# Turning gathered token rows on VectorE by way of DRAM, instead of on TensorE, for experts two to seven

## The chip, the core and the metric

The program runs on one NeuronCore of a Trainium2 chip. The metric is the device time of one execution in microseconds (us), the median of three. The engines are TensorE (PE: matrix products; PEld: its weight loads), VectorE (DVE), ScalarE (ACT), GpSimd (POOL) and SyncE (SP, which here only issues DMAs). Each works through its own instructions in order and waits on semaphores; DMAs are issued from an engine's queue and land later.

## The reference, cut to what matters

```python
# attention: B, S, D = 8, 2496, 256; d_qk = 64
scores = scale * np.matmul(z, z.transpose(0, 2, 1))
attn = np.maximum(scores, 0.0) ** 2
x = (u * np.matmul(attn, v)).reshape(B * S, D)
# mixture of experts: E, F = 8, 1024
do_compute = x @ w_skip > 0
e_idx = np.argmax(xc @ w_gate, axis=1)          # xc = x[do_compute]
gate_w = softmax(xc @ w_gate)[e_idx]
for e in range(E):
    h = np.maximum(xc[mask] @ w1[e], 0.0)       # mask = e_idx == e
    y[mask] = gate_w[mask, None] * (h @ w2[e])
out[do_compute] = xc + y                        # the other tokens keep x
```

All is float32. About half of the 19968 tokens are computed, 1073 to 1502 for each expert.

## The kernel before

**Attention phase (to about 1250 us).** It is tiled by batch and by 512 queries. The rows x are stored in DRAM (`xr`) and the routing scatters every computed token's number and gate into its expert's list (`lst`). The change does not touch this phase.

**Expert phase.** The experts, counted here from 0 to 7 as in the code (e0 to e7), come one after the other. An expert's tokens are taken in *pairs* of two tiles of 128. Each product is split into float32r high and low parts (`xh`/`xl`, `w1h`/`w1l`, `hh`/`hl`). `unit` computes 256 to 512 tokens: it forms h in PSUM (tile `psh`), ACT takes the relu into `hh`, DVE the rest into `hl`, PE multiplies by w2 into `y`, DVE adds x and POOL scatters the rows to `out`. The first NFIX = 3 pairs of each expert are *fixed units*. What is left is done in one arm of a switch (`tc.Switch`), chosen by the expert's count: its code is entered by a branch on each engine. Weights of expert e + 1 are brought by SP (`raw`), cast on ACT and subtracted on POOL (`w1l`, `w2t`), in eight pieces over the fixed units of expert e.

**A pair's way before.** `fetch` gathers its rows by two indirect DMAs of POOL (tiles `xgf` for pairs 0 to 2, `xgu` for later ones); before them DVE copies the row numbers (`go`). `turn_pe` transposes it on PE with four products against an identity into PSUM (`pst`); ACT casts it into xh and DVE subtracts for xl. Turned pairs lie in `xt` (two buffers in turn) and `xtf` (pair 0 of an expert from e1 on).

**What sets the order.** The instruction order is the code's (`manual_schedule`). `unit` runs a list of parts: for a fixed unit h0, h1, h2, h3, y0, y1, then the rest of y. `fills` maps a part's number to the steps written behind it. At 3 the next pair is turned. In the third unit (i = 2) pair 4 is turned at 5 and pair 0 of the next expert at 7, the last thing before the switch. The pieces of the weights stand at 1, 3 and 5.

Of the kernel before, what the change touches and what calls it, by code (L numbers as in the profile page):

```python
# [8 lines left out]
F32 = mybir.dt.float32  # L9
# [35 lines left out]
def f32(ap):  # L45
    return ap.bitcast(F32)
# [3 lines left out]
def attn_moe(ctx, tc, zT, uT, v, wg, w1, w2, cst, pad, out):  # L50
# [4 lines left out]
    nc = tc.nc  # L55
# [593 lines left out]
    def turn_pe(xg, xt, n=2, o=0, rows64=False):  # L649

        if rows64:
            ps = spare()[:, 0, :].rearrange("p (d q) -> p d q", d=2)
        else:
            ps = ps_acc.tile([P, 2, 2 * P], F32, name="pst", tag="acc")
        for t in range(n):
            for d in range(2):
                nc.tensor.transpose(ps[:, d, t * P : (t + 1) * P], xg[:, t, d * P : (d + 1) * P], ident)  # L657
        xh, xl = (x[:, :, o : o + n * P] for x in xt)
        nc.scalar.copy(xh, ps[:, :, : n * P])
        nc.vector.tensor_sub(xl, ps[:, :, : n * P], f32(xh))  # L660

    def unit(e, hw, ids, xg, xt, fills=(), own=False, lead=3):


# [320 lines left out]
    def add(fills, *slots):  # L985
        for k, f in slots:
            fills.setdefault(k, []).append(f)

    def rows(e, i):
        return lambda: fetch(ids_of(e, i), pair(e, i))  # L990

    for e in range(E):
        more = e + 1 < E
        wq = load_w(e + 1, nc.gpsimd if e else nc.vector) if more else []
        narms = NARM + (2 if e == 0 else 1)
        for i in range(NFIX):
            fills = {}
            if e:

                add(fills, (1, rows(e, i + 3)), (3, lambda: turn_pe(pair(e, i + 1), turned(e, i + 1))))  # L1000
                if e == 1 and i == 0:
                    add(fills, (0, rows(1, 2)))
                if more:
                    add(fills, (4, rows(e + 1, i)))
                if i == 0 and e + 2 < E:
                    add(fills, (6, lambda: load_ids(idts[e + 2], e + 2, 2 * NSTAT)))
                add(fills, *zip((1, 3, 5), wq[3 * i : 3 * i + 3]))
            elif i == 0:
                add(fills, (0, lambda: turn_pe(pair(0, 1), turned(0, 1))))
                add(fills, (1, gates), (1, logits), (1, route), (2, counts), (2, gate), (2, rows0), (2, rows1),  # L1010
                    (2, store), (4, store), (5, end_routes), (6, end_lists))
                add(fills, *zip((0, 2), left))
            elif i == 1:
                add(fills, (1, end_counts), (3, lambda: turn_pe(pair(0, 2), turned(0, 2))), (4, rows(0, 3)), (6, rows(0, 4)))
                add(fills, *zip((1, 3, 5), wq[:3]))
            else:
                add(fills, (1, rows(1, 0)), (3, rows(0, 5)), (4, lambda: turn_pe(pair(0, 3), turned(0, 3))),
                    (5, rows(1, 1)), (6, lambda: load_ids(idts[2], 2, 2 * NSTAT)))
                add(fills, *zip((1, 2, 3, 5, 6), wq[3:]))
            if more and i == NFIX - 1:  # L1020
                add(fills, (7, lambda: turn_pe(pair(e + 1, 0), turned(e + 1, 0))))
            if i == NFIX - 1:

                add(fills, (5, lambda: turn_pe(pair(e, NFIX + 1), turned(e, NFIX), 2, 2 * P)))
                n = nc.values_load(fin["arm"][0:1, e : e + 1], min_val=0, max_val=narms - 1)
                add(fills, (1, lambda: tc.switch_hint({g: n for g in ENGINES}, narms, label="rest%d" % e)))
            ids = ids_of(e, i) if e else idt_e[:, 2 * i : 2 * i + 2, :]
            xg = pair(e, i)
            unit(e, 4, ids, [xg[:, 0, :], xg[:, 1, :]], turned(e, i), fills)


        for arm in tc.Switch(n, narms, hint="rest%d" % e):
            ws = widths(arm) if arm <= NARM else []
            if arm > NARM:
                for i in range(NFIX):
                    xg = fetch(ids_of(0, i), xgs["u"][i])
# [3 lines left out]
            i, there = NFIX, NFIX + 2  # L1040
            for j, hw in enumerate(ws):
                fills = {}
                after = ws[j + 1 :]
                nxt = i + -(-hw // 4)
                while there < min(i + 3, end - 1):
                    there += 1
                    add(fills, (1, rows(e, there)))
                if after:
                    xt = xts[(NFIX + j + 1) % 2]
                    add(fills, (3, lambda nxt=nxt, xt=xt: turn_pe(pair(e, nxt), xt)))  # L1050
                    if after[0] > 4:
                        add(fills, (5, lambda nxt=nxt, xt=xt: turn_pe(pair(e, nxt + 1), xt, 2, 2 * P)))
                w = -(-hw // 2)
                xg = [pair(e, i + t // 2)[:, t % 2, :] for t in range(w)]
                unit(e, hw, ids_of(e, i, w), xg, xts[(NFIX + j) % 2], fills, not more and not after, 3 if j else 4)
                i = nxt
            if arm >= NARM:
                ce = nc.values_load(fin["cnt"][0:1, e : e + 1], min_val=0, max_val=N)
                with tc.For_i((NSTAT if arm == NARM else NFIX) * UT, ce, UT) as tok:
                    it = op.tile([P, 2, 2], I32, name="it", tag="it")  # L1060
                    nc.sync.dma_start(
                        it, lst[bass.ds(tok + e * CAP, UT), :].rearrange("(k p) c -> p k c", p=P)
                    )
                    xg = fetch(it, xgs["u"][0])
                    turn_pe(xg, xts[0])
                    unit(e, 4, it, [xg[:, 0, :], xg[:, 1, :]], xts[0])


# [53 lines left out]
```

## Time and profile before

| what | value |
|---|---|
| time, median of 3 runs | 1735.2 us (1734.55 to 1735.56) |
| profiled execution | 1747.08 us, of which the span is 1745.1 us |
| PE busy | 1724.1 us, 99% |
| VectorE busy | 1206.2 us, 69% |
| ScalarE busy | 1112.6 us, 64% |
| POOL busy | 520.1 us, 30% |
| granted TensorE clock | 0.996 |
| HBM | 184.21 MB read, 136.02 MB written |

Shares are averages over two unlike phases. In the expert phase PE works on; DVE and ACT are busy about 40% and a third of the time, POOL over half. A row of the timeline gives start, duration, engine, line, operation, out<-in, and in brackets the idle time before it and what ended it. A row with a count at the end (x4) is several instructions in one, from the first's start to the last's end. In the chain of waits a row is start, duration and what the end of the program hung on then; "issue" there is time in which an engine waited for nothing that the profile shows. SPq is a DMA's issue on SP.

### The profile page before, as it was taken

The page shows a single profiled execution, that of the slowest core. Times are in us where ns is not written, and L with a number is a line of the kernel's source. Part 1 is how long each engine was busy: PE and PEld are TensorE (multiplying, and loading weights), DVE is VectorE, ACT ScalarE, POOL GpSimd, SP SyncE. Part 2 cuts the span into 40 slices and gives each one's busy share as a digit, 9 for nine tenths or more (in the row PEclk, how much of TensorE's full clock was granted, in tenths as well). Part 3 has the DMA queues.
Part 4 walks back from the last instruction along what each step waited for, and adds up shares of the span by engine and source line. Part 5 has one row for each costly group of instructions (what it writes and reads, how often), then busy time and mean ns, then how long its engine had stood idle before and what let it go on. Part 6 is the DMA issues. An engine that isn't in the chain of part 4 may idle for free.

```text
span 1745.1 us, 39255 instructions
## 1 busy us (share of the span) xinstructions
PE 1724.1 (99%) x15474; PEld 1537.9 (88%) x15474; DVE 1206.2 (69%) x1976; ACT 1112.6 (64%) x1409; POOL 520.1 (30%) x516
## 2 busy tenths in 40 slices
PE   9999999999999999999999999999989999999998
PEld 7888789988888998888889888888889999999997
DVE  6877877887887888788788878877744334443333
ACT  7877877787687778768777876877333333333321
POOL 1103213212211321231132023112446556635731
PEclk9999999999999999999999999999999999999999
DMA  5576699579858957985895799589543323322210
GB/s 179 152 203 193 151 247 281 144 211 258 236 146 243 277 147 204 272 239 146 236 262 162 207 261 254 140 225 250 149 111 84 90 83 106 100 61 86 86 42 26
DMA packets 408113, 303.29 MB, mean 174 GB/s; under 512 B 202768, under 2 KB 346001, under 8 KB 407152
## 3 DMA queue, kind: packets, MB, share of 16 engines
q1 hardware_dynamic: 393728, 276.37, 57.6%
q0 software_dynamic: 13632, 22.99, 4.7%
q8 instruction: 137, 2.24, 0.5%
q14 instruction: 184, 1.51, 0.3%
q10 hardware_dynamic: 432, 0.18, 0.0%
HBM read 184.21 MB, written 136.02 MB: 183 GB/s over the span
## 4 chain that ended last, share of the span: by engine, by line
PE 90%; DMA 3%; issue 3%; DVE 1%; ACT 1%; another core or an unknown queue 1%; POOL 1%; SPq 0%; POOLq 0%; DVEq 0%; ACTq 0%
PE acc L419 59%; PE y L710 10%; PE psh L691 10%; PE ps L302 8%; DMA out<-o,idt 2%; PE psm L491 1%; PE pst L657 1%; PE ps L285 0%; DMA kept<-rt 0%; DVE hl L697 0%; DVE al L390 0%; DMA raw<-in_v 0%; ACT ah L386 0%; DMA xgu<-xr,go 0%
## 5 line engine op out<-in xcount | busy, mean ns | idle before, releaser
L419 PE MATMUL acc<-ah,vh 64*128 64x512 f32 (+1 forms) x3120 | 643.7, 384 | 0.9 <-DVE ah L386 0.8
L419 PE MATMUL acc<-ah,vl 64*128 64x512 f32 (+1 forms) x3120 | 629.4, 383 | 0.0
L390 DVE TENSOR_TENSOR al<-r,ah 128x1024 fp32r<-128x1024 f32 (+1 forms) x400 | 479.8, 1206 | 135.2 <-ACT ah L386 114.9
L419 PE MATMUL acc<-al,vh 64*128 64x512 f32 (+1 forms) x3120 | 499.0, 383 | 0.6 <-DVE al L390 0.2
L590 POOL DMA_INDIRECT lst<-pair,dest x160 | 202.4, 1265 | 773.5 <-DVE dest L588 688.7
L386 ACT CAST ah<-r 128x1024 fp32r<-128x1024 f32 (+1 forms) x356 | 363.5, 1032 | 90.4 <-PE acc L419 41.8
L419 PEld LDWEIGHTS acc<-ah,vh 64*128 64x128 f32 x3120 | 329.3, 185 | 48.1 <-DVE ah L386 1.6
L419 PEld LDWEIGHTS acc<-ah,vl 64*128 64x128 f32 x3120 | 329.6, 185 | 41.6 <-DVE vl L122 0.3
L419 PEld LDWEIGHTS acc<-al,vh 64*128 64x128 f32 x3120 | 312.5, 184 | 51.0 <-DVE al L390 7.7
L376 ACT ACTIVATE r<-ps 128x1024 f32<-128x1024 f32 (+1 forms) x224 | 228.0, 1018 | 134.6 <-PE ps L302 116.1
L696 ACT ACTIVATE hh<-psh 128x512 fp32r<-128x512 f32 (+2 forms) x172 | 96.3, 572 | 287.6 <-PE psh L691 233.1
L377 ACT ACTIVATE r<-r 128x1024 f32<-128x1024 f32 (+1 forms) x224 | 236.3, 1055 | 7.1
L710 PE MATMUL y<-w2t,hh 128*128 128x256 f32 (+1 forms) x1328 | 235.8, 280 | 0.0
L697 DVE SCALAR_TENSOR_TENSOR hl<-psh,hh 128x512 fp32r<-128x512 f32 (+2 forms) x172 | 110.0, 655 | 151.9 <-ACT hh L696 121.3
L319 DVE STREAM_TRANSPOSE rt<-r 128x512 f32<-128x512 f32 x304 | 197.4, 688 | 10.2 <-DMA kept<-rt 9.4
L710 PEld LDWEIGHTS y<-w2t,hh 128*128 128x128 f32 (+1 forms) x1328 | 201.1, 186 | 1.8 <-issue 0.6
L691 PE MATMUL psh<-xt,w1h 128*128 128x256 f32 (+3 forms) x896 | 185.8, 304 | 8.6 <-DVE hl L697 5.9
L710 PE MATMUL y<-w2t,hl 128*128 128x256 f32 (+1 forms) x664 | 184.8, 278 | 0.8 <-DVE hl L697 0.7
L691 PEld LDWEIGHTS psh<-xt,w1h 128*128 128x128 f32 x896 | 142.4, 190 | 14.5 <-DVE hl L697 7.3
L691 PE MATMUL psh<-xt,w1l 128*128 128x256 f32 (+3 forms) x448 | 135.3, 302 | 0.0
L742 POOL DMA_INDIRECT out<-o,idt x77 | 76.5, 994 | 167.6 <-DVE o L739 132.5
L710 PEld LDWEIGHTS y<-w2t,hl 128*128 128x128 f32 (+1 forms) x664 | 123.0, 185 | 1.2 <-DVE hl L697 1.2
(197 smaller groups left out, 1750.6 us busy)
## 6 DMA issues: line engine op xcount, KB each, us to landing
kept<-rt SPq DMA_DIRECT2D x242, 256.0 KB
r<-kept SPq DMA_DIRECT2D x90, 512.0 KB
r<-kept SPq DMA_DIRECT2D x62, 448.0 KB
raw<-in_v SPq DMA_DIRECT2D x80, 256.0 KB
ut<-in_uT SPq DMA_DIRECT2D x32, 512.0 KB
xr<-xrow SPq DMA_DIRECT2D x128, 128.0 KB
out<-xr SPq DMA_DIRECT2D x32, 512.0 KB
raw<-in_w SPq DMA_DIRECT2D x64, 256.0 KB
```

Source lines behind the costliest of these rows:

```text
L302: nc.tensor.matmul(to, k[h, o : o + P], queries(ci, q, h, n), start=(m == 0), stop=(m == 2))
L319: nc.vector.transpose(t[:, :, 32 * k : 32 * k + 32].rearrange("p (k a) i -> p a k i", k=4), r[:, x, :].rearrange("p (a k i) -> p a k i", a ...
L376: nc.scalar.activation(r[:, :, :n], ps[:, :, :n], AF.Relu, scale=isc)
L377: nc.scalar.activation(r[:, :, :n], r[:, :, :n], AF.Square)
L386: (nc.scalar.copy if on_act(ci, p) else nc.vector.tensor_copy)(h_, r_)
L390: nc.vector.tensor_sub(l_, r_, f32(h_))
L419: nc.tensor.matmul(acc[t][:, :n], w[h, x, dd], a[h, x, :n], start=(first and t not in halves[:m]), stop=(last and t not in halves[m + 1 :]),)
L590: put = nc.gpsimd.indirect_dma_start(out=lst, out_offset=bass.IndirectOffsetOnAxis(ap=dest[:, t : t + 1], axis=0), in_=pair[:, t, :], in_o ...
L691: nc.tensor.matmul(ps[:, j * W : (j + 1) * W], wt[:, a, o : o + P], x[:, d, :W], start=(m == 0), stop=(m == 5),)
L696: nc.scalar.activation(hh[:, : G * W], ps[:, : G * W], AF.Relu)
L697: nc.vector.scalar_tensor_tensor(hl[:, : G * W], ps[:, : G * W], 0.0, f32(hh[:, : G * W]), op0=ALU.max, op1=ALU.subtract)
L710: nc.tensor.matmul(ys[t], h[:, tt], w2t[f][:, k, :], start=(f == 0 and m == 0 and t % share == 0), stop=(f == NF - 1 and m == 2), skip_gro ...
```

## The change

For experts from FAR = 2 on, a pair is no longer turned by PE. SP writes the gathered rows to a DRAM buffer (`far`, one for each pair and each parity of e) and reads them back with four DMAs as 32-row blocks that lie across partitions (`blocks`, into `blk`, or into `xgu` number 2 for pair 0). DVE transposes all 32x32 blocks in one instruction (`turn_dve`, into `xraw`); cast and subtraction stay, but read SBUF in place of PSUM. The columns come out in another order, and w1 is reordered on the host to match.

The gathers of a pair stand in other fills: two pairs in each fixed unit as before, but pairs 3 and 4 of the own expert in unit 0, pair 5 and the next expert's pair 0 in unit 1, the next expert's pairs 1 and 2 in unit 2. Expert 1 gathers pair 5 only if its arm wants it. Each write and each reading of blocks has a place of its own in the fills.

```diff
+FAR = 2
...
+    far = [[dram.tile([UT, D], F32, name="far%d%d" % (k, i)) for i in range(NSTAT)] for k in range(2)]
...
+    def blk_of(i):
+        return blk[i % 2][:, : UT // 32] if i else xgs["u"][2].rearrange("p t (m f) -> p (t m) f", f=64)
+
+    def blocks(e, i):
+        src = far[e % 2][i].rearrange("(m i) (b f) -> b i m f", i=32, b=4)
+        for b in range(4):
+            nc.sync.dma_start(blk_of(i)[32 * b : 32 * b + 32], src[b])
+
+    def to_far(e, i):
+        return lambda: nc.sync.dma_start(far[e % 2][i].rearrange("(t p) d -> p t d", p=P), pair(e, i))
+
+    def turn_dve(e, i, xt, o=0):
+        raw = zp.tile([P, 2 * D], F32, name="xraw", tag="zf", bufs=3)
+        nc.vector.transpose(
+            raw.rearrange("p (d m i) -> p m d i", d=2, i=32),
+            blk_of(i).rearrange("p m (d j) -> p m d j", d=2),
+        )
+        xh, xl = (x[:, :, o : o + UT] for x in xt)
+        r = raw.rearrange("p (d q) -> p d q", d=2)
+        nc.scalar.copy(xh, r)
+        nc.vector.tensor_sub(xl, r, f32(xh))
...
     def pair(e, i):
-        return xgs["f"][NFIX * (e % 2) + i] if i < NFIX else xgs["u"][i % 4]
+        if e < FAR:
+            return xgs["f"][NFIX * (e % 2) + i] if i < NFIX else xgs["u"][i % 4]
+        j = i % (NFIX + 3)
+        if j < NFIX:
+            return xgs["f"][NFIX * (e % 2) + j]
+        return xgs["u"][j % 4] if e % 2 else more_rows[j - NFIX]
...
+    def turn(e, i, xt, o=0):
+        return (lambda: turn_dve(e, i, xt, o)) if e >= FAR else (lambda: turn_pe(pair(e, i), xt, 2, o))
...
-                add(fills, (1, rows(e, i + 3)), (3, lambda: turn_pe(pair(e, i + 1), turned(e, i + 1))))
+                if e < FAR:
+                    if i < NFIX - 1:
+                        add(fills, (1, rows(e, i + 3)))
+                else:
+                    add(fills, (0, to_blocks(e, i + 1)))
+                    if i == 0:
+                        add(fills, (0, to_far(e, 2)), (1, rows(e, 3)), (4, rows(e, 4)))
+                    elif i == 1:
+                        add(fills, (1, to_far(e, 3)), (1, rows(e, 5)), (4, to_far(e, 4)))
+                    else:
+                        add(fills, (1, to_blocks(e, 4)), (3, to_far(e, 5)), (6, to_blocks(e, 5)))
+                add(fills, (3, turn(e, i + 1, turned(e, i + 1))))
...
-                if more:
-                    add(fills, (4, rows(e + 1, i)))
+                if more and i == 1:
+                    add(fills, (3, rows(e + 1, 0)))
+                if more and i == 2:
+                    add(fills, (0, to_far(e + 1, 0)), (1, rows(e + 1, 1)), (4, to_blocks(e + 1, 0)),
+                        (4, rows(e + 1, 2)), (6, to_far(e + 1, 1)))
...
             if more and i == NFIX - 1:
-                add(fills, (7, lambda: turn_pe(pair(e + 1, 0), turned(e + 1, 0))))
+                add(fills, (7, turn(e + 1, 0, turned(e + 1, 0))))
...
+    w1 = np.concatenate([moe_w1[:FAR], moe_w1[FAR:, cols]])
```

In the arms the same steps are put in for pairs from 6 on, and a loop for very large counts is adapted.

**On SP**, in the fixed units of e3 (raw: the next expert's weights; idt5: a list; far12: pair 2 of an odd expert; far00: pair 0 of the next, even one), from unit 0 on, before:

```order
L97 DMA raw_40508<-in_w1 128x512
L97 DMA raw_40546<-in_w2 128x512
L631 DMA idt5_206<-lst_88 128x16x2
L97 DMA raw_40629<-in_w2 128x512
L97 DMA raw_40676<-in_w2 128x512
L97 DMA raw_40716<-in_w2 128x512
```

and now, from the last weights of unit 1 to the end of unit 2:

```order
L99 DMA raw_40797<-in_w2 128x512
L677 DMA far14_101<-xgu_18280 128x2x256
L99 DMA raw_40830<-in_w2 128x512
L1081 TENSOR_LOAD arm_18550
L1081 ISA x2
L674 DMA blk_18285<-far13_100 32x8x64 x4
L677 DMA far00_89<-xgf_17860 128x2x256
L674 DMA blk_18284<-far14_101 32x8x64 x4
L1082 SWITCH_STRIDE
L1082 ISA
L1082 BRANCH_PREFETCH_HINT
L677 DMA far15_102<-xgu_18281 128x2x256
```

The weights' last load is now ahead of the blocks of pair 3, and the write of the next expert's pair 0 (far00) ahead of the blocks of pair 4 (far14); behind far15 follow the four reads of far00.

**On POOL**, in unit 1 of e3 (xgu: the own expert's later pairs; xgf: the next expert's), before:

```order
L639 DMA xgu<-xr,go 128x256 x2
L153 TENSOR_TENSOR w1l<-raw,w1h 128x512
L159 TENSOR_TENSOR w2t<-raw,w2t 128x256 x2
L639 DMA xgf<-xr,go 128x256 x2
L159 TENSOR_TENSOR w2t<-raw,w2t 128x256 x2
L742 DMA out<-o,idt_204 19968x256 x2
```

and now:

```order
L641 DMA xgu<-xr,go 128x256 x2
L155 TENSOR_TENSOR w1l<-raw,w1h 128x512
L641 DMA xgf<-xr,go 128x256 x2
L161 TENSOR_TENSOR w2t<-raw,w2t 128x256 x4
L771 DMA out<-o,idt_220 19968x256 x2
```

The number of gathers is the same; the xgf pair, which was pair 1 of the next expert and is now its pair 0, went ahead of one piece of w2t.

**On DVE**, the end of unit 2 of e3, before:

```order
L660 TENSOR_TENSOR xt_17848<-pst,xt_17848 128x2x256
L637 COPY go<-idt_205 128x2
L660 TENSOR_TENSOR xt_17848<-pst,xt_17848 128x2x256
L660 TENSOR_TENSOR xtf<-pst,xtf 128x512
L739 SCALAR_TENSOR_TENSOR o<-y,idt_204,xgf 128x256 x2
```

and now:

```order
L689 TENSOR_TENSOR xt_17864<-xraw,xt_17864 128x2x256
L639 COPY go<-idt_221 128x2
L682 STREAM_TRANSPOSE xraw<-blk 128x8x2x32
L689 TENSOR_TENSOR xt_17864<-xraw,xt_17864 128x2x256
L682 STREAM_TRANSPOSE xraw<-xgu 128x8x2x32
L689 TENSOR_TENSOR xtf<-xraw,xtf 128x512
L768 SCALAR_TENSOR_TENSOR o<-y,idt_220,xgf 128x256 x2
```

The transposes of pair 4 and of the next expert's pair 0 (read from xgu number 2, where its blocks are put) stand in DVE's queue ahead of the third unit's output and of the branch.

More of the change, by code (lines that the diff above doesn't have):

```diff
@@ L928, in attn_moe @@
     row_tiles("u", 4)
+    blk += [xp.tile([P, QC // 32, D // 4], F32, name="blk", tag="xrow") for _ in range(2)]
+    more_rows += [xp.tile([P, 2, QC], F32, name="xgx", tag="ut", bufs=3)[:, 0].rearrange("p (t f) -> p t f", t=2) for _ in range(3)]
     xtf += [zp.tile([P, 2, 2 * P], F32R, name="xtf", tag="zl", bufs=ZBUFS) for _ in range(2)]
@@ L1008, in attn_moe @@
             elif i == 0:
-                add(fills, (0, lambda: turn_pe(pair(0, 1), turned(0, 1))))
+                add(fills, (0, turn(0, 1, turned(0, 1))))
                 add(fills, (1, gates), (1, logits), (1, route), (2, counts), (2, gate), (2, rows0), (2, rows1),
@@ L1013, in attn_moe @@
             elif i == 1:
-                add(fills, (1, end_counts), (3, lambda: turn_pe(pair(0, 2), turned(0, 2))), (4, rows(0, 3)), (6, rows(0, 4)))
+                add(fills, (1, end_counts), (3, turn(0, 2, turned(0, 2))), (4, rows(0, 3)), (6, rows(0, 4)))
                 add(fills, *zip((1, 3, 5), wq[:3]))
             else:
-                add(fills, (1, rows(1, 0)), (3, rows(0, 5)), (4, lambda: turn_pe(pair(0, 3), turned(0, 3))),
+                add(fills, (1, rows(1, 0)), (3, rows(0, 5)), (4, turn(0, 3, turned(0, 3))),
                     (5, rows(1, 1)), (6, lambda: load_ids(idts[2], 2, 2 * NSTAT)))
@@ L1039, in attn_moe @@
             end = NFIX + -(-sum(ws) // 4)
-            i, there = NFIX, NFIX + 2
+            i, there = NFIX, NFIX + 2 - (e == 1)
             for j, hw in enumerate(ws):
@@ L1046, in attn_moe @@
                     there += 1
-                    add(fills, (1, rows(e, there)))
+                    add(fills, (1, rows(e, there)), *([(3, to_far(e, there))] if e >= FAR else []))
                 if after:
                     xt = xts[(NFIX + j + 1) % 2]
-                    add(fills, (3, lambda nxt=nxt, xt=xt: turn_pe(pair(e, nxt), xt)))
-                    if after[0] > 4:
-                        add(fills, (5, lambda nxt=nxt, xt=xt: turn_pe(pair(e, nxt + 1), xt, 2, 2 * P)))
+                    for k in range(2 if after[0] > 4 else 1):
+                        if e >= FAR and nxt + k > NFIX + 2:
+                            add(fills, (2 + 2 * k, to_blocks(e, nxt + k)))
+                        add(fills, (3 + 2 * k, turn(e, nxt + k, xt, 2 * P * k)))
                 w = -(-hw // 2)
@@ L1063, in attn_moe @@
                     )
-                    xg = fetch(it, xgs["u"][0])
-                    turn_pe(xg, xts[0])
+                    xg = xs = fetch(it, xgs["u"][2 if e >= FAR else 0])
+                    if e >= FAR:
+                        xs = zp.tile([P, 2, D], F32, name="xs", tag="zf", bufs=3)
+                        for t in range(2):
+                            nc.vector.tensor_copy(
+                                xs[:, t].rearrange("p (d b j) -> p b d j", d=2, b=4),
+                                xg[:, t].rearrange("p (b d j) -> p b d j", b=4, d=2),
+                            )
+                    turn_pe(xs, xts[0])
                     unit(e, 4, it, [xg[:, 0, :], xg[:, 1, :]], xts[0])
```

7 lines of the change are left out of this document (5 added, 2 removed).

## The prediction

> **What bounds the kernel now.** I read the page first, then the matrix engine's waits from 1230 us on, then the transposes by source line, then the queues around one expert in the timeline.
>
> ```profile
> span 1745.1 us, 39255 instructions
> ...
> PE 1724.1 (99%) x15474; PEld 1537.9 (88%) x15474; DVE 1206.2 (69%) x1976; ACT 1112.6 (64%) x1409; POOL 520.1 (30%) x516
> ```
> ```profile
> PE psh L691 <- DVE hl L697: 5.9, 4, 2.8
> ```
> ```profile
> L657 PE MATMUL pst<-ident,xgf x72: 270/273/273, 1349.0 to 1686.5; 128*128 128x128 f32 x72
> L657 PE MATMUL pst<-ident,xgu x68: 272/272/273, 1401.2 to 1710.1; 128*128 128x128 f32 x68
> ```
> ```profile
> 1697.62 0.28 PE L691 MATMUL psh<-xt,w1l 128*128 128x256 f32 x1
> 1697.74 0.60 PE L657 MATMUL pst<-ident,xgu 128*128 128x128 f32 x4
> 1698.09 0.37 PE L710 MATMUL y<-w2t,hh 128*128 128x256 f32 x1
> ```
>
> TensorE (PE) is busy 99% of the span. In the expert phase its one real wait is for VectorE's hl, four times, 5.9 us in all. The transposes of experts 2 to 7 are these 72 + 68 = 140 (the window starts behind expert 1's own), 35 pairs of four. Four hold the engine from 1697.74 to 1698.09, 0.35 us. That is all the edit can take off directly: 35 x 0.35 = 12.3 us.
>
> What the pairs wait for instead is a chain of queues, so I looked at one expert (e3, window 1430 to 1488) for GpSimd (POOL).
>
> ```profile
> 1430.00:1488.00 58.00, 57.36 (x460) 56.30 (x459) 22.70 (x41) 18.43 (x37) 33.43 (x35) 1.00 0.33 91
> ```
> ```profile
> 1452.49 1.02 POOL L639 DMA_INDIRECT xgu<-xr,go  x1 [0.30 <-issue]
> 1453.53 1.32 POOL L153 TENSOR_TENSOR w1l<-raw,w1h 128x512 fp32r<-128x512 f32 x1
> 1454.77 1.45 POOL L159 TENSOR_TENSOR w2t<-raw,w2t 128x256 fp32r<-128x256 f32 x2
> 1456.38 1.01 POOL L639 DMA_INDIRECT xgf<-xr,go  x1 [0.16 <-issue]
> 1457.70 1.01 POOL L639 DMA_INDIRECT xgf<-xr,go  x1 [0.30 <-issue]
> ```
>
> VectorE (22.70 of 58 us) and ScalarE (18.43) have room. POOL, though, works through the fixed units without a pause: each row starts 0.16 to 0.30 us behind the one before it. Its gathers come when the queue reaches them, not when a unit asks. Today that is hidden, since a gathered pair is needed a unit or more later.
>
> **The change part by part.** *Removed:* the 35 x 0.35 us on PE.
>
> *Added on VectorE:* 35 transposes of 128x512.
>
> ```profile
> L319 DVE STREAM_TRANSPOSE rt<-r x304: 662/686/714, 49.6 to 1209.3; 128x512 f32<-128x512 f32 x152
> ```
>
> 35 x 0.69 = 24 us, spread over six experts (4 us in each 58, where 35 us are idle): hidden. ScalarE's cast and VectorE's subtraction stay and cost the same.
>
> *Added on SyncE (SP):* per pair one write of 256 KB and four reads of 64 KB, all behind the weight loads in one queue, each with its own wait. The fixed code's last turn decides, the next expert's pair 0: VectorE and ScalarE cannot enter the switch's arm before it. Today's price of that entry, in the chain of waits for e3:
>
> ```profile
> 1466.94 3.68 issue
> ...
> 1470.83 0.55 ACT hh L696
> ...
> 1471.48 0.64 DVE hl L697
> ...
> 1472.16 1.48 PE psh L691 x6
> ```
>
> ScalarE's cast of the pair (below, 1466.71) is followed by 3.68 us of branch, then hh, hl, and only then PE's fifth product at 1472.16, where PE has already waited. So the end of an expert's fixed part hangs on the start of that cast, not on PE's work. Savings of PE ahead of it are returned if the cast is late. Casts now, and the second gather row in whose neighbourhood the next expert's pair 0 will be gathered (e4 and e5 read like e3):
>
> ```profile
> 1349.61 0.59 ACT L659 CAST xtf<-pst 128x512 fp32r<-128x512 f32 x1 [2.60 <-PE pst L657]
> ```
> ```profile
> 1408.18 0.59 ACT L659 CAST xtf<-pst 128x512 fp32r<-128x512 f32 x1 [2.59 <-PE pst L657]
> ```
> ```profile
> 1466.71 0.59 ACT L659 CAST xtf<-pst 128x512 fp32r<-128x512 f32 x1 [2.16 <-PE pst L657]
> ```
> ```profile
> 1641.96 0.59 ACT L659 CAST xtf<-pst 128x512 fp32r<-128x512 f32 x1 [2.55 <-PE psh L691]
> ```
> ```profile
> 1341.37 1.31 POOL L153 TENSOR_TENSOR w1l<-raw,w1h 128x512 fp32r<-128x512 f32 x1
> ```
> ```profile
> 1401.85 1.01 POOL L639 DMA_INDIRECT xgf<-xr,go  x1 [0.31 <-issue]
> ```
> ```profile
> 1633.30 1.01 POOL L639 DMA_INDIRECT xgf<-xr,go  x1 [0.30 <-issue]
> ```
>
> Prices of the links, from the nearest rows:
>
> ```profile
> 1584.50 3.82 DMA xgu<-xr,go
> ```
> ```profile
> 1487.64 0.98 POOL L742 DMA_INDIRECT out<-o,idt  x1 [0.30 <-issue]
> 1490.76 0.98 POOL L742 DMA_INDIRECT out<-o,idt  x1 [2.14 <-DMA out<-o,idt]
> ```
> ```profile
> 675.58 1.81 SPq L781 DMA_DIRECT2D kept<-rd  x4
> ```
> ```profile
> 1259.40 1.96 SPq L469 DMA_DIRECT2D xr<-xrow  x4
> 1263.54 0.49 SPq L465 DMA_DIRECT2D out<-xr  x1
> ```
> ```profile
> 1342.70 0.33 SPq L97 DMA_DIRECT2D raw<-in_w  x1
> ```
> ```profile
> 1345.81 0.72 ACT L158 CAST w2t<-raw 128x256 fp32r<-128x256 f32 x2 [1.97 <-DMA raw<-in_w]
> ```
>
> A gather lands 3.1 us (scatter, 1487.64 to 1490.76) to 3.8 us (1584.50) after it is issued; I take 3.3. A plain SP transfer of 256 KB takes 0.33 us to issue and 3.1 us to its reader (1342.70 to 1345.81). Four block transfers of the new shape, 32x8x64, take SP 1.81 us. Until all four have landed it is at most 4.1 us (1259.40 to 1263.54, for 112 KB each); below, no less than the 1.8 us of issuing. I take 3.7, near the upper row, since the new ones are the same but smaller.
>
> *The walk for e3.* In POOL's new order the next pair 0 is gathered ahead of the two w2t rows (1.44 us): its second gather starts at 1457.70 - 1.44 = 1456.26 and lands at 1459.56. SP's write of it issues until 1459.9; behind it stand pair 4's four block reads (1.81), then the branch hint and the write of pair 5 (0.85 together, two issues and register work, an estimate from the 0.33). The block reads of the next pair 0 start at 1462.6 and land at 1466.3; VectorE turns it (0.69) and the cast starts at 1467.0, against 1466.71: 0.3 us later. Row to cast is thus 9.3 us. By it e2's cast starts at 1411.15 (now 1408.18: +3.0), e6's at 1642.6 (+0.6), e4's and e5's are +0.3 and +0.1. Expert 1 gathers one pair less (2 x 1.32 us of POOL), so its w1l row ends at 1340.0 and the next pair 0's second gather starts at 1341.5; then 3.3 + 0.33 + 3.1 (write landed) + 3.7 + 0.75 gives 1352.7 against 1349.61: +3.1. Sum +7.4 us.
>
> PE's savings that remain are those behind the last late cast: the arms of e4 and e6 (two turns each) and e7's five, 9 x 0.35 = -3.2 us. In e7 no weights follow, so its SP queue has no waits for POOL's subtractions. The other 26 turns' 9.1 us are handed to the wait.
>
> *A cost that the rows show only elsewhere:* the new subtraction reads two operands from SBUF where the old one read PSUM. Where VectorE does so now beside POOL:
>
> ```profile
> L263 POOL CAST zqh<-zh x47: 334/632/1642, 7.6 to 1202.9; 128x512 fp32r<-128x512 f32 x31, 128x256 fp32r<-128x256 f32 x8, 128x192 fp32r<-128x192 f32 x8
> ```
> ```profile
> L390 DVE TENSOR_TENSOR al<-r,ah x400: 1049/1224/1991, 10.6 to 1242.9; 128x1024 fp32r<-128x1024 f32 x107, 128x896 fp32r<-128x896 f32 x27
> ```
> ```profile
> L153 POOL TENSOR_TENSOR w1l<-raw,w1h x24: 1277/1298/1318, 1329.8 to 1629.2; 128x512 fp32r<-128x512 f32 x24
> ```
>
> A POOL cast goes from 0.63 to 1.64 us, a VectorE subtraction from 1.05 to 1.99, while w1l in the expert phase varies by 0.04. Per expert one turn lies ahead of the gather in POOL's way (0 to 0.7 us) and one subtraction stands ahead of the branch behind a POOL row (0 to 1.3). I take 0.5 together, a quarter of 2.0, since a collision needs both to meet: 6 x 0.5 = +3 us.
>
> [...]
>
> Sum: +7.4 - 3.2 + 3 = +7.2 us on the profiled execution's 1747.1 us. That execution is 12 us above the median of the runs shown, 1735.2; carried over unchanged, 1742.4 us. About 0.2% (3.5 us) is what a measurement here can tell from no change.
>
> **The rivals.** *The cover holds (faster).* If the next pair 0's blocks land 2.5 us earlier per expert than in my walk, the casts never come later than PE, and PE keeps all 12.3 us: 1722.9. It decides from a chain of 9.3 down to about 7 us. For it: SP issues at 0.33 us would save 0.5 us on each set of four, and 1.8 us is the floor of their landing. Against it: POOL's unbroken queue, and pair 4's reads standing in SP behind a gather that isn't theirs.
>
> *The two cancel.* A chain 0.7 to 1.5 us shorter than 9.3 in the six experts, or no collisions, brings the sum to between -2 and +3: about 1736.
>
> *Collisions on most rows.* Every one of the two meetings per expert costs its whole 0.7 and 1.3 us: 7.4 - 3.2 + 6 x 2.0 = +16.2, 1751.4. For it: L263's 1.64. Against it: beside the transposes of the attention phase POOL has had no such dense queue, so no row shows the dense case.
>
> *VectorE becomes the bound:* 22.7 + 4 of 58 us speak against it; no chance of its own.
>
> **How the numbers follow.** My forecast, late casts by 0 to 3 us: 0.42, 1742.4, its own range 1738 to 1748. Cover holds: 0.21, 1722.9. Cancel: 0.20, 1736. Collisions: 0.17, 1751.4. Range: the links' bounds together move the chain by -2.4 to +1.3 us (landing -0.2 and +0.5, issue -1.0, blocks -1.2 to +0.4, turn and branch hint 0 to +0.4), six times; the low end 1727 leaves out the best of the cover's cases, the high end 1757 takes the collisions with longer landings. Faster 0.21, same 0.20, slower 0.59.
>
> **What the profile would show.** Right: no pst on PE from e2 on, 140 fewer; xtf casts 35 to 39 us behind each expert's first product, released by VectorE behind a DMA; the wait of PE's psh on hl grown from 5.9 us to 12 or more, at the arms' entries; in SP's waits the write of a pair waiting for the gather. Wrong: casts as early as now or earlier and PE's span down by 12 us (chain overpriced); w1l rows of 1.5 us and more (collisions); waits at the starts of units 1 and 2 instead of the arms (the turns of pairs 2 and 3 late, which in my walk have some 0.5 to 1 us to spare).

## The result and the profile after

The changed kernel takes 1759.26 us (median of 4 runs, 1757.47 to 1763.13) against 1735.38 us before (1734.55 to 1737.09, same chip): a ratio of 1.0140, with a 95% interval of 1.0125 to 1.0155. It is slower by 23.9 us. Forecast were 1742.4 us and a range of 1727 to 1757. Measured beside the experiments below, the kernel before took 1733 to 1743 us (medians); so it is their ratios to it that are compared, not the times.

The head of the page and a window of the expert phase, of the kernel after:

```profile
span 1755.6 us, 39353 instructions
...
PE 1715.0 (98%) x15334; PEld 1533.7 (87%) x15334; DVE 1233.5 (70%) x2010; ACT 1115.3 (64%) x1409; POOL 521.9 (30%) x514
```
```profile
1300.00:1700.00 400.00, 370.70 (x2905) 361.31 (x2904) 174.34 (x308) 124.25 (x243) 210.19 (x216) 0.97 0.46 122
```

And the same window of the kernel before (columns: window, length, busy time and instructions of PE, PEld, DVE, ACT, POOL, granted clock, DMA share, GB/s):

```profile
1300.00:1700.00 400.00, 396.45 (x3223) 389.93 (x3223) 156.85 (x290) 126.22 (x252) 215.17 (x221) 1.00 0.28 80
```

The 140 products are gone (15474 to 15334), but in 400 us of the expert phase TensorE is idle for 29.3 us in place of 3.6, and its mean clock is 0.97 in place of 1.00. The two profiled executions differ by only 10.4 us (1747.08 and 1757.47), since the one before lies 11.7 us above its median: its e1 begins at 1313.65 us, that of the kernel after at 1302.23, and no step ahead of e1 is changed. From the start of e1's first product to that of the last of all it is 424.2 us before and 446.6 after, +22.4, close to the 23.9 of the medians.

TensorE's waits in the kernel after, from 1300 us on (us in total, times, longest):

```profile
PE psh L720 <- issue: 10.3, 3, 5.5
PE psh L720 <- DVE hl L726: 7.6, 2, 4.8
PE y L739 <- ACT hh L725: 7.4, 2, 3.9
PE psh L720 <- DVE xt L689: 2.7, 3, 1.5
PE y L739 <- DVE hl L726: 1.3, 2, 0.8
```

That is 29.3 us; before it was 3.5. All of the waits over 2 us lie at the arms' entries, but they are of two kinds. Three of them in the timeline, e2, e3 and e4:

```profile
1404.15 1.48 PE L720 MATMUL psh<-xt,w1h 128*128 128x512 f32 x2 [5.48 <-issue]
...
1466.32 1.42 PE L720 MATMUL psh<-xt,w1h 128*128 128x448 f32 x2 [4.63 <-issue]
...
1532.73 0.51 PE L739 MATMUL y<-w2t,hh 128*128 128x256 f32 x2 [3.51 <-ACT hh L725]
```

In e4 (and e1, e5, e6) it is a product in the middle of the arm's first unit that waits for ScalarE or VectorE, which have not come through the branch: the wait of the forecast. In e2 and e3 it is the arm's *first* product, and it reads xt. "issue" names no releaser, but VectorE's rows at that place and ScalarE's do (e3):

```profile
1464.86 0.71 DVE L682 STREAM_TRANSPOSE xraw<-blk 128x512 f32<-128x512 f32 x1 [4.29 <-DMA blk<-far]
1466.25 0.69 DVE L689 TENSOR_TENSOR xt<-xraw,xt 128x512 fp32r<-128x512 f32 x1 [0.68 <-ACT xt L688]
1467.17 0.71 DVE L682 STREAM_TRANSPOSE xraw<-xgu 128x512 f32<-128x512 f32 x1 [0.22 <-issue]
```
```profile
1465.60 0.62 ACT L688 CAST xt<-xraw 128x512 fp32r<-128x512 f32 x1 [5.23 <-DVE xraw L682]
```

The cast of pair 4, the turn's second step, ends at 1466.22, and TensorE goes on at 1466.32. The arms of e2, e3 and e5 take pairs 3 and 4 as one unit of up to 512 columns, so their first products need pair 4's turn; those of e4 and e6 begin with pair 3 alone (256 columns). In e5 the first products wait 0.88 us for pair 4's low part, and the long wait, 4.82 us, comes behind them, on hl. The queues that this turn hung on, SP's and GpSimd's:

```profile
1457.89 0.39 SPq L677 DMA_DIRECT2D far<-xgf  x1
1458.38 1.93 SPq L674 DMA_DIRECT2D blk<-far  x4
1460.86 0.39 SPq L677 DMA_DIRECT2D far<-xgu  x1
1461.43 3.48 SPq L674 DMA_DIRECT2D xgu<-far  x4
```
```profile
1452.48 1.00 POOL L641 DMA_INDIRECT xgf<-xr,go  x1 [0.30 <-issue]
```

The write of the next pair 0 went out at 1457.89, 5.4 us behind its second gather; pair 4's reads stood behind it, and from their first issue to VectorE's transpose passed 6.5 us (1458.38 to 1464.86). Those of the next pair 0 took at most 5.7 (1461.43 to 1467.17), of which 3.48 were spent issuing. Its transpose did not wait for them: VectorE was busy with pair 4's subtraction until 1466.94, and by the semaphores in the trace the last of the four had landed at 1466.58, 5.1 us behind the first issue.

### The profile page after: what moved, and what is told of

The parts are those of the page before. It is cut to its first block, busy times and chain, and to the rows that moved or that the text cites. A ratio compares the mean times of both kernels' runs of the same rounds, so it can differ in the third digit from the quotient of the medians.

```text
span 1755.6 us, 39353 instructions
## 1 busy us (share of the span) xinstructions
PE 1715.0 (98%) x15334; PEld 1533.7 (87%) x15334; DVE 1233.5 (70%) x2010; ACT 1115.3 (64%) x1409; POOL 521.9 (30%) x514
## 4 chain that ended last, share of the span: by engine, by line
PE 82%; DMA 8%; issue 4%; POOL 2%; ACT 2%; DVE 1%; SPq 1%; POOLq 0%; DVEq 0%; ACTq 0%
PE acc L421 57%; PE ps L304 8%; PE y L739 7%; PE psh L720 7%; DMA xgf<-xr,go 4%; DMA out<-o,idt 2%; PE psm L493 1%; SPq L674 1%; DMA xgu<-far 1%; PE ps L287 0%; DMA blk<-far 0%; DVE al L392 0%; ACT ah L388 0%; POOL w2t L161 0%; ACT r L378 0%
## 5 line engine op out<-in xcount | busy, mean ns | idle before, releaser
L592 POOL DMA_INDIRECT lst<-pair,dest x160 | 206.4, 1290 | 762.7 <-DVE dest L590 733.0
L739 PEld LDWEIGHTS y<-w2t,hh 128*128 128x128 f32 (+1 forms) x1328 | 205.9, 189 | 9.2 <-ACT hh L725 7.8
L720 PEld LDWEIGHTS psh<-xt,w1h 128*128 128x128 f32 x896 | 144.5, 192 | 28.8 <-issue 11.3
```

The costliest lines, as they stand in the source:

```text
L592: put = nc.gpsimd.indirect_dma_start(out=lst, out_offset=bass.IndirectOffsetOnAxis(ap=dest[:, t : t + 1], axis=0), in_=pair[:, t, :], in_o ...
L720: nc.tensor.matmul(ps[:, j * W : (j + 1) * W], wt[:, a, o : o + P], x[:, d, :W], start=(m == 0), stop=(m == 5),)
L739: nc.tensor.matmul(ys[t], h[:, tt], w2t[f][:, k, :], start=(f == 0 and m == 0 and t % share == 0), stop=(f == NF - 1 and m == 2), skip_gro ...
```

## The experiments

Theory 1: the way through DRAM costs time only because turned pairs come late at the arms, held by a late gather in SP's queue. Its rivals: VectorE's added work (A), the traffic (B), the branch (C), and the half clock behind each gap (theory 3).

### Without the way through DRAM

```diff
     def blocks(e, i):
-            nc.sync.dma_start(blk_of(i)[32 * b : 32 * b + 32], src[b])
...
     def turn_dve(e, i, xt, o=0):
-            blk_of(i).rearrange("p m (d j) -> p m d j", d=2),
+            pair(e, i).rearrange("p t (m f) -> p (t m) f", f=64).rearrange("p m (d j) -> p m d j", d=2),
```

The writes to far are left out too.

> The changed kernel without its way through DRAM: VectorE transposes the gathered rows where they lie, nothing is written to far and no blocks are read (the rows come out in a wrong order, so the result is not the reference's; all the counts of instructions on TensorE, VectorE and ScalarE stay). Theory 1 (the time is lost in the chain write, block reads, cast that hangs behind a late gather in SP's queue): with the chain gone the 35 x 0.35 = 12.3 us of TensorE come out whole, about 1723 us (1720 to 1727), the xtf casts no later than before's, no gap of TensorE over 2.5 us at an arm's entry. Rival A (VectorE's work itself, its subtraction on two SBUF operands beside GpSimd): 1735 us or more, hl still waited for at the arms' entries.

Measured: 1730.18 against 1741.49 us, ratio 0.994 (0.9924 to 0.9957), 11.3 us faster. TensorE's waits from 1300 us on:

```profile
PE psh L720 <- DVE hl L726: 3.9, 2, 2.5
PE psh L720 <- issue: 1.3, 2, 0.9
```

So theory 1 holds in the main: nearly all of the 12.3 us come out, and VectorE's transposes and its subtraction on two SBUF operands cost little in this run. One wait reached 2.5 us, in e5.

### The traffic alone

```diff
     def turn(e, i, xt, o=0):
-        return (lambda: turn_dve(e, i, xt, o)) if e >= FAR else (lambda: turn_pe(pair(e, i), xt, 2, o))
+        return lambda: turn_pe(pair(e, i), xt, 2, o)
...
-    w1 = np.concatenate([moe_w1[:FAR], moe_w1[FAR:, cols]])
+    w1 = moe_w1
```

> The changed kernel with all its writes to far, its block reads and its order of the gathers, but TensorE turns the pairs again, from the gathered rows; nobody reads the blocks. Theory 1: a turn waits for the gather alone, which in the changed kernel has landed some 8 us before the cast, so 1735 to 1738 us, like the kernel before. Rival B (the added DMA traffic, 35 x 0.5 MB, slows the weight loads, gathers and scatters so far that units wait for them whoever turns the rows): 1745 us or more, with TensorE gaps inside the units.

Measured: 1743.26 against 1741.49 us, ratio 1.0012 (1.0002 to 1.0021). That is theory 1's number: all of the writes, reads and moved gathers together cost 2 us if nobody waits for them.

### The next pair 0 turned in the arm

```diff
-                add(fills, (7, turn(e + 1, 0, turned(e + 1, 0))))
+                if e + 1 < FAR:
+                    add(fills, (7, turn(e + 1, 0, turned(e + 1, 0))))
...
                 fills = {}
+                if j == 0 and more and e + 1 >= FAR:
+                    add(fills, (5 if hw > 4 else 3, turn(e + 1, 0, turned(e + 1, 0))))
```

> The changed kernel, but the turn of the next expert's pair 0 (transpose, cast, subtraction) stands in the arm's first unit instead of ahead of the branch; every DMA stays where it is. Theory 1: VectorE and ScalarE enter the arm after pair 4's turn instead, whose transpose starts at 1464.9 in e3 against 1467.2 for the next pair 0, so each arm's entry comes 2 to 2.5 us earlier; over six experts 12 to 15 us, and fewer stretches of half clock: 1742 to 1747 us. Rival C (the entry hangs on the branch itself, or on SP's queue): 1757 to 1760 us, as the changed kernel.

Measured: ratio 1.0086 (1.0063 to 1.0108), 1755.57 against 1741.49 us. About 9 us of the 24 come back, two thirds of what I expected; rival C, by which nothing would come back (a ratio of 1.012 or more), is out. The reason is in the waits:

```profile
PE psh L720 <- issue: 8.0, 4, 5.0
PE psh L720 <- DVE o L768: 3.4, 5, 0.9
```

The 5.0 us stand in e2, at the arm's first product, as in the kernel after: pair 4's turn, which this edit does not touch. With the next run it showed me the second wait.

### Pair 4's reads ahead of the next pair 0's write

```diff
-                        add(fills, (1, to_blocks(e, 4)), (3, to_far(e, 5)), (6, to_blocks(e, 5)))
+                        add(fills, (0, to_blocks(e, 4)), (3, to_far(e, 5)), (6, to_blocks(e, 5)))
```

> The changed kernel, but in SP the four block reads of pair 4 stand ahead of the write of the next expert's pair 0, which waits there for its gather (3.5 us in e3). Theory 1 in my walk's form (SP's order holds the chain: 1.9 us of pair 4's reads lie between the write and the reads of the next pair 0): the chain behind the gather gets 1.9 us shorter, the xtf casts come 1.5 to 2 us earlier, six times 1.5 to 2 us plus some half clock: 1.006 to 1.009 of before. Rival E (landing decides: the write must land 2.2 to 3 us before the first read may go, and pair 4's reads were hidden in that): casts at most 0.5 us earlier, 1.012 to 1.015.

Measured: 1755.53 against 1733.50 us, ratio 1.013 (1.011 to 1.015). The number is rival E's, its reason is not. VectorE's transposes in e3 (pair 3, pair 4, next pair 0):

```profile
1458.98 0.71 DVE L682 STREAM_TRANSPOSE xraw<-blk 128x512 f32<-128x512 f32 x1 [1.12 <-DMA blk<-far]
1461.06 0.70 DVE L682 STREAM_TRANSPOSE xraw<-blk 128x512 f32<-128x512 f32 x1
1466.27 0.71 DVE L682 STREAM_TRANSPOSE xraw<-xgu 128x512 f32<-128x512 f32 x1 [3.00 <-DMA xgu<-far]
```

Pair 4 is turned 3.8 us earlier, and the wait of the arm's first product is nearly gone (4.63 to 0.42 us); but the next pair 0 is only 0.9 us earlier, and now its wait shows behind the branch:

```profile
1471.71 0.73 PE L720 MATMUL psh<-xt,w1h 128*128 128x448 f32 x2 [3.46 <-DVE hl L726]
```

The two waits lay side by side.

### Both edits together

```diff
-                        add(fills, (1, to_blocks(e, 4)), (3, to_far(e, 5)), (6, to_blocks(e, 5)))
+                        add(fills, (0, to_blocks(e, 4)), (3, to_far(e, 5)), (6, to_blocks(e, 5)))
...
+                if j == 0 and more and e + 1 >= FAR:
+                    add(fills, (5 if hw > 4 else 3, turn(e + 1, 0, turned(e + 1, 0))))
```

> The changed kernel with two edits that were run apart: the next expert's pair 0 is turned in the arm's first unit (alone: 1.0086 of before, with TensorE still standing 5.3 us in e2 and 1.9 + 1.2 us in e3 for pair 4's turn), and pair 4's block reads stand in SP ahead of the next pair 0's write (alone: 1.013, where pair 4's turn came 3 to 4 us earlier and the branch was late instead). Theory 1, mended (two late turns side by side, the shorter wait hidden under the longer): together more than the sum of both, since neither hides the other: another 3 us in e2, 2 to 3 in e3, 1 in e5 and some half clock off the first, 1.003 to 1.006. Rival F (the two edits touch the same wait): no better than the first alone, 1.008 to 1.010.

Measured: 1744.50 against 1742.54 us, ratio 1.001 (0.9994 to 1.0026). Apart, the two edits brought 0.5% and 0.1%; together 1.3%, almost the whole loss. That is the test of two waits that hide each other, and better than expected.

### Smaller pieces or larger ones

```diff
-        src = far[e % 2][i].rearrange("(m i) (b f) -> b i m f", i=32, b=4)
+        src = far[e % 2][i].rearrange("(b p t) d -> b p (t d)", b=4, t=2)
```

> The changed kernel with the same number of block reads, the same bytes, places and waits, but each reads 32 pieces of 2 KB in place of 256 pieces of 256 B (the rows come out in a wrong order, so the result is not the reference's). Theory 2 (the small pieces make the reads' landing long: in e3 5.7 us from the first issue to the last landing of four reads, where I had 3.7, and one issue of 2.0 us in place of 0.45): the reads land about 2 us earlier, the casts come 2 us earlier, six times: 1.004 to 1.009 of before. Theory 1 alone (queue and gather, whatever the pieces): 1.012 to 1.015.

Measured: 1753.23 against 1733.50 us, ratio 1.0116 (1.0095 to 1.0137). In e3 pair 4's reads then took 4.6 us from first issue to transpose in place of 6.5, the next pair 0's 4.7 in place of 5.1 to 5.7. The interval overlaps that of the changed kernel, so a part of 0.2% is likely but not shown; the size of the pieces is not the main cause.

### Idle products in the gaps

```diff
+            if k == lead - 1:
+                for _ in range(busy):
+                    nc.tensor.matmul(
+                        ys[0], xh[:, 0, : rows_of[0]], w2t[0][:, 0, :], start=True, stop=True, skip_group_check=True
+                    )
```

> The changed kernel with 32 idle products of 128x256 added on TensorE in the first unit of an arm (experts 1 to 6), where TensorE now stands still 3.2 to 5.8 us for VectorE and ScalarE; at 0.11 us each they fill 3.5 us of it. Nothing else changes. Theory 3 (each of these gaps also halves the granted clock for 3.4 to 6.8 us behind it, which costs 1.5 to 2.2 us of products each): the half clock goes at most arms, and the time falls by up to 6 x 1.7 = 10 us, to 1.008 to 1.011 of before. Rival D (the half clock in the profile costs nothing, or the idle products only delay the real ones): 1.014 or more.

Measured: ratio 1.0172 (1.0155 to 1.0189), 1763.53 against 1733.50 us. Rival D's number, but the run was not the test I meant. In e2, e3 and e6 TensorE waited ahead of the arm's first product, so the idle products came behind that and only delayed the rest. Where they fell into the gap, as in e4, the clock did stay up; the same window of the run and of the kernel after:

```profile
1530.00:1540.00 10.00, 9.27 (x82) 9.08 (x81) 5.99 (x10) 3.38 (x7) 4.04 (x4) 1.00 0.42 120
```
```profile
1530.00:1540.00 10.00, 6.45 (x42) 6.24 (x43) 5.86 (x10) 3.31 (x6) 2.03 (x2) 0.83 0.44 142
```

There e1, e4 and e5 became 0.8, 1.2 and 1.5 us shorter (first product to first product). So a stretch of half clock costs at least about a microsecond, a rough price: it is from one execution, in which e2 became 3.7 us longer, and the idle products take time of their own.

### Earlier gathers: three attempts

*The next pair 0 as a third pair in unit 0.*

```diff
+                if more and i == 0:
+                    add(fills, (6, rows(e + 1, 0)))
                 if more and i == 1:
-                    add(fills, (3, rows(e + 1, 0)))
+                    add(fills, (3, rows(e + 1, 1)), (5, to_far(e + 1, 0)))
...
-                    add(fills, (0, to_far(e + 1, 0)), (1, rows(e + 1, 1)), (4, to_blocks(e + 1, 0)),
-                        (4, rows(e + 1, 2)), (6, to_far(e + 1, 1)))
+                    add(fills, (0, to_blocks(e + 1, 0)), (1, rows(e + 1, 2)), (4, turn(e + 1, 0, turned(e + 1, 0))),
+                        (6, to_far(e + 1, 1)))
```

> The changed kernel with the next expert's pair 0 gathered in unit 0 (as third pair there), its pair 1 in unit 1, pair 2 in unit 2; pair 0 is written at the end of unit 1, its blocks are read at the start of unit 2 and turned at fill 4, ahead of pair 4. Nothing in SP waits for a gather that has just been issued. Theory 1: both last turns have more than half a unit to spare, the casts fall to or below before's times, the gaps at the arms' entries return to about before's (0 to 2.2 us) and the half clock goes: 1722 to 1728 us, faster than before. Rival B (landings that are long under the added traffic wherever they stand): 1740 us or more.

Measured: 1764.29 against 1741.49 us, ratio 1.0135 (1.0118 to 1.0152). Wrong: no better than the changed kernel. SP in e3:

```profile
1459.08 0.38 SPq L677 DMA_DIRECT2D far<-xgf  x1
1461.78 0.35 SPq L99 DMA_DIRECT2D raw<-in_w  x1
1463.22 1.43 SPq L674 DMA_DIRECT2D blk<-far  x4
```

A third pair of gathers made GpSimd late; SP held the write for the gather and then the weight load for GpSimd's subtraction, and twelve block reads came in a row from 1463.22. Pair 4 was turned at 1473.49.

*The gathers in the order of before.*

```diff
+                add(fills, (1, rows(e, i + 3)))
...
+                if more:
+                    add(fills, (4, rows(e + 1, i)))
+                    if i == 1:
+                        add(fills, (1, to_far(e + 1, 0)), (6, to_blocks(e + 1, 0)))
+                    if i == 2:
+                        add(fills, (4, turn(e + 1, 0, turned(e + 1, 0))), (6, to_far(e + 1, 1)))
```

> All turns on VectorE by way of DRAM, but the gathers in the order of the kernel before (in unit i: pair i + 3 of the own expert, then pair i of the next one). The next expert's pair 0 is thus gathered in unit 0, written in unit 1 at 1, read at the end of unit 1 and turned in unit 2 at 4; pair 4 is gathered in unit 1, written at the start of unit 2, read at 2 and turned at 5. No unit gathers three pairs, so GpSimd's subtractions, and with them the weight loads that stand ahead of the reads in SP, are no later than before. Theory 1 (the loss is the chain behind a late gather in SP's queue): what is left is TensorE's saving without the chain (the run without DRAM: ratio 0.994) and the traffic's own cost (the run with idle traffic: 1.001), so 0.993 to 0.998 of before, no gap at an arm's entry over 3 us. Rival B (the way through DRAM is too long wherever it stands, or SP's queue with 35 x 5 more transfers is full): 1.005 or more, as the run with the earlier gathers (1.0135).

Measured: 1756.68 against 1733.50 us, ratio 1.0132 (1.0116 to 1.0149). Wrong again, and for one clear reason (VectorE, then TensorE, in e3):

```profile
1457.77 0.70 DVE L682 STREAM_TRANSPOSE xraw<-xgu 128x512 f32<-128x512 f32 x1
...
1464.15 0.71 DVE L682 STREAM_TRANSPOSE xraw<-blk 128x512 f32<-128x512 f32 x1 [4.30 <-DMA blk<-far]
```
```profile
1465.61 0.71 PE L720 MATMUL psh<-xt,w1h 128*128 128x448 f32 x1 [6.52 <-issue]
```

The next pair 0 is early now (1457.77), and pair 4, gathered half a unit later than in the changed kernel, holds TensorE longer than there (4.63).

*Everything half a unit or more ahead.* Pair 3 is gathered in the expert before, pair 4 and the next pair 0 in unit 0; their reads follow in the middle of unit 1.

```diff
+                elif i == 0:
+                    add(fills, (0, to_blocks(e, 1)), (0, to_far(e, 2)), (1, to_far(e, 3)), (1, rows(e, 4)),
+                        (4, to_blocks(e, 2)))
+                elif i == 1:
+                    add(fills, (0, to_far(e, 4)), (0, to_blocks(e, 3)), (1, rows(e, 5)), (4, to_blocks(e, 4)))
...
+                if more and i == 1:
+                    add(fills, (1, to_far(e + 1, 0)), (4, rows(e + 1, 1)), (4, to_blocks(e + 1, 0)))
...
+            if e < FAR + 1 or k != 4:
+                bring(k + ahead)
```

> All turns on VectorE by way of DRAM, with everything half a unit or more earlier: an expert's pair 3 is gathered in the third unit of the expert before, its pair 4 in unit 0 with the next expert's pair 0, pair 5 with the next pair 1 in unit 1 (two pairs in each unit, as before). In SP pair 4 and the next pair 0 are written at the start of unit 1 and read in its middle, ahead of the last weight load, which stood in front of them waiting for GpSimd; both are turned in unit 2 at 4 and 5. Theory 1, as the runs so far have mended it (two turns are late in the changed kernel: pair 4's, which the first product of an arm over 256 tokens reads, and the next pair 0's, which VectorE and ScalarE must have done before they branch; bringing forward one of them only, as the run with the gathers of before did, leaves the time with the other): by the run without DRAM (0.994) and the idle traffic (1.001), 0.993 to 0.998 of before; TensorE's gaps at the arms under 2 us each. Rival B (a way through DRAM beside the weight loads is late wherever it stands, since SP's queue is held elsewhere): 1.003 or more.

Measured: ratio 1.0093 (1.0075 to 1.0111), 1757.58 against 1742.54 us. That is a miss, with rival B's number. The last two lines were a mistake of mine: they put a weight load behind eight block reads. VectorE's waits show it:

```profile
DVE hl L727 <- ACT w2t L161: 16.2, 5, 4.9
```

ScalarE stood waiting to cast the weights, with hh behind it, and hl and the three turns behind that. In the changed kernel VectorE has no such wait.

### Two versions that beat the kernel before

The first takes both edits, reads pair 3's blocks at the end of unit 1, and turns pair 3 in unit 2 at 1, pair 4 at 3, and the next pair 0 in the arm's last unit. The second takes the last schedule above, the weight loads where they were, and turns at 1, 3 and 5 (the first two lines below are against that schedule, the others, which both versions have, against the changed kernel):

```diff
-            if e < FAR + 1 or k != 4:
-                bring(k + ahead)
+            bring(k + ahead)
...
-                add(fills, (3, turn(e, i + 1, turned(e, i + 1))))
+                add(fills, (1 if e >= FAR and i == 2 else 3, turn(e, i + 1, turned(e, i + 1))))
...
-                add(fills, (5, turn(e, NFIX + 1, turned(e, NFIX), 2 * P)))
+                add(fills, (3 if e >= FAR else 5, turn(e, NFIX + 1, turned(e, NFIX), 2 * P)))
```

> The run with both edits (1.001), with three more places changed: pair 3's blocks are read at the end of unit 1 in place of the start of unit 2 and turned in unit 2 at 1 in place of 3; pair 4 is turned at 3 in place of 5; and the next pair 0 is turned in the arm's last unit instead of its first. What was left of TensorE's gaps there was 2.4 us in e2 and 0.9 in e3 (pair 4's turn 2.1 us behind pair 3's, since transpose, cast and subtraction of a turn follow each other), 2.2 in e4 and 0.9 + 1.9 in e6 (the next pair 0's turn ahead of the arm's own). Theory 1, mended (only the wait for a late turn costs): up to 8 us of these go, 0.996 to 0.999 of before. Rival (the traffic and SP's queue take it elsewhere): 1.000 to 1.003.

> The run with everything gathered, written and read earlier (1.0093), with its weight loads at their old places (there one load had been put behind eight block reads, and ScalarE's cast of the weights stood 3.7 us and more for it in unit 2, with hh, hl and all turns behind it), and with pair 3 turned in unit 2 at 1, pair 4 at 3, the next pair 0 at 5. Theory 1, mended: blocks landed before they are turned, three turns of 2.1 us each done by the end of unit 2: 0.993 to 0.999 of before. Rival B (a third wait takes the place: SP holds the weight loads or the reads): 1.003 or more.

Measured: the first 1726.09 against 1733.04 us, ratio 0.9953 (0.9939 to 0.9966); the second 1719.52, ratio 0.9915 (0.9901 to 0.9929), 13.5 us faster than before. Both are a little better than their ranges, and rival B, by which a third wait takes the place, is out. In the second the one stretch of half clock that the kernel before has in its expert phase (in e5) is gone too. TensorE's waits in the second from 1300 us on, and VectorE in its e3:

```profile
PE psh L720 <- DVE hl L726: 2.0, 2, 1.6
PE y L739 <- DVE hl L726: 0.7, 1, 0.7
```
```profile
1450.42 0.69 DVE L682 STREAM_TRANSPOSE xraw<-blk 128x512 f32<-128x512 f32 x1
1451.80 0.69 DVE L689 TENSOR_TENSOR xt<-xraw,xt 128x512 fp32r<-128x512 f32 x1 [0.69 <-ACT xt L688]
1452.48 0.71 DVE L682 STREAM_TRANSPOSE xraw<-xgu 128x512 f32<-128x512 f32 x1
```

None of these transposes waits for a DMA. In the changed kernel VectorE's transposes waited for their blocks 31.6 us in all (waits from 1300 to 1700 us):

```profile
DVE xraw L682 <- DMA blk<-far: 22.8, 12, 4.3
...
DVE xraw L682 <- DMA xgu<-far: 8.8, 3, 4.0
```

The same view of the second version has no wait of a transpose at all. These are the same 35 ways through DRAM with the same traffic (36 writes and 144 block reads in both); what cost 24 us in the change was when each step came, not the way itself.

## Why the prediction was wrong, step by step

**The saving on TensorE, 12.3 us:** right. 140 products fewer, and 11.3 us in the run without DRAM.

**VectorE's 24 us hidden:** right. Its busy time grew by 27.3 us (1206.2 to 1233.5); the run without DRAM has that work and none of the loss.

**"The fixed code's last turn decides":** this step failed. It decides at the entries of e1, e4, e5 and e6. In e2 and e3 the arm's first product waits (5.48 and 4.63 us) for the turn before it, pair 4's. My walk had pair 4 only as something that fills SP's queue, and never asked who reads it. Both edits together, against each alone, show that there are two waits.

**The lengths of the links:** sized too small, and this is the term that put the number wrong. In e3 the gather took 5.4 us to the write, not 3.3; four block reads 5.1 and 6.5 us to their landing, not 3.7. The casts of the next pair 0, counted from the expert's first product, came later by 2.8, 5.6, 4.1, 2.8, 4.8 and 3.1 us in e1 to e6, 23.2 in sum, where I had +7.4. In e3 that is 4.1 us in place of 0.3. With +23.2 my sum would have been +23.0 (23.2 - 3.2 + 3), against the 22.4 measured from e1 on. Even with these lengths a hit would have been luck in part: in e2 and e3 TensorE's wait is another one, which lies beside the late cast and is of similar length, and the half clock stands nowhere in the sum. All four of my cases used the short links, so all lay below the time. The four reads took 1.4 and 2.8 us longer than my 3.7 where reads, writes and gathers were under way together (DMA share 0.64 in e3's gap, below). The traffic's mean cost is nonetheless 2 us in the whole run: a late landing costs only where somebody waits.

**The savings kept behind the last late cast, -3.2 us:** about right where it can be seen: e7 is 2.1 us shorter (69.0 to 66.9), with five turns of 0.35.

**Collisions, +3 us:** there are some, but not on the rows I named. GpSimd's rows in the expert phase of the kernel after, by source line:

```profile
L155 POOL TENSOR_TENSOR w1l<-raw,w1h x24: 1282/1299/1316, 1317.9 to 1638.1; 128x512 fp32r<-128x512 f32 x24
```
```profile
L161 POOL TENSOR_TENSOR w2t<-raw,w2t x48: 713/737/1197, 1330.6 to 1652.0; 128x256 fp32r<-128x256 f32 x48
```

and the latter's of the kernel before:

```profile
L159 POOL TENSOR_TENSOR w2t<-raw,w2t x48: 715/743/766, 1342.6 to 1643.1; 128x256 fp32r<-128x256 f32 x48
```

w1l is as before. Two of 48 w2t rows take 1.19 us in place of 0.74, each beside one of the new subtractions; 4 of 35 subtractions take 1.0 to 2.5 us in place of 0.69, 3.0 us more together. The longest lies beside a w1l row, and TensorE waits for it at the start of e5's third unit:

```profile
1577.84 2.47 DVE L689 TENSOR_TENSOR xt<-xraw,xt 128x512 fp32r<-128x512 f32 x1 [0.69 <-ACT xt L688]
...
1578.46 1.28 POOL L155 TENSOR_TENSOR w1l<-raw,w1h 128x512 fp32r<-128x512 f32 x1
...
1580.36 0.39 PE L720 MATMUL psh<-xt,w1h 128*128 128x256 f32 x1 [1.53 <-DVE xt L689]
```

So a part of the +3 us is real, 1.5 us of it at one place. The rival with collisions on most rows, 6 x 2.0 = 12 us, is out: 31 of the 35 subtractions and 46 of the 48 w2t rows took their usual time, and the others came to 3.9 us more. In the second version a subtraction of e3 takes 1.06 us too (at 1447.63), and it is the fastest kernel of all.

**The half clock:** missing from the sum. TensorE in e3 of the kernel after, around its gap:

```profile
1461.41:1466.32 4.91, 0.28 (x3) 0.11 (x2) 0.78 (x2) 0.62 (x1) 4.43 (x7) 0.90 0.64 167
1466.32:1472.10 5.78, 5.78 (x15) 4.85 (x16) 3.15 (x6) 1.61 (x3) 2.30 (x3) 0.50 0.54 157
1472.10:1480.00 7.90, 7.90 (x51) 7.53 (x50) 3.31 (x6) 2.20 (x5) 0.17 (x1) 1.00 0.61 169
```

The clock is 0.50 for all of the 5.8 us behind the gap. Before there was one such stretch in the expert phase (3.4 us, in e5), after there are six, 27.3 us in all. Each of the six, 3.4 or 6.8 us long, lies at one of the waits of the arms' entries, five of 3.5 to 5.5 us and one of 2.8. So these waits of TensorE cost more than their length.

The sum as it came: waits 29.3 - 3.5 = +25.8, products -12.3, together +13.5 of the +22.4. At the 0.8 to 1.5 us of the idle products, five more stretches of half clock would be 4 to 8 us. The trace gives a closer price. From one start to the next, the products in the six stretches took 11.3 us more than the same products usually take in the rest of the expert phase (1.4 to 2.9 us for each stretch), and those in the one stretch before 1.5 us more. With this difference of +9.7 the sum is +23.2, which is 0.8 us too much.

**What should have shown it:** the write waiting for its gather did appear (SP, 24.0 us in 8 waits), and 140 fewer products. The casts came 38.7 to 41.5 us behind each first product where I had said 35 to 39. The wait on hl grew to 8.9 us by its own rows, not 12; ScalarE's hh and the rows with "issue" took the rest. The direction and the place, the arms' entries, were right; the time was 2.3 us above my high end, and the change, +23.9 us, was more than three times the +7.2 of my sum.

## What to carry to other kernels

When a short step is replaced by a long chain of transfers, walk every turned piece to the first instruction that reads it, not only the last one of the code: two late pieces side by side hide each other, and mending one alone shows little. In a queue like SP's here, where pair 4's reads stood behind a write that went out 5.4 us behind its gather, each transfer must be issued when what it waits for has long landed; the same work went from 1.4% slower to 0.85% faster by the places of its gathers, writes, reads and turns alone. And price a new wait of the matrix engine with the slow clock behind it: here 1.4 to 2.9 us of products at each of the six waits of 2.8 to 5.5 us.

## What was unexpected of the hardware

- A single DMA issue on SP, usually 0.45 us here, took 1.0 to 2.8 us some two times in each expert. In most experts one stands behind the load of a list (idt), as it did before (1.7 to 1.9 us); the other is one of the block reads: the first of the four at 1461.43 took 2.0 us, the four 3.48. Why it is so, no run here tells.
- The length of a wait on TensorE does not tell here whether half clock follows. In the kernel before, the clock was 0.50 for 3.4 us behind a wait of 1.9 us in e5, and stayed at 1.00 behind one of 2.8 us in e0; in the run without DRAM it stayed at 1.00 behind one of 2.5 us. In the changed kernel all six waits from 2.8 us on had it.
